# Attention and experts kernel: batch 1's reciprocals spread by 64x64 products in two banks, with a new written-out order

## The chip, the cores and the metric

The program runs on one core of one Trainium2 chip. The metric is the device time of one execution in microseconds (us); lower is better. TensorE (PE) does the matrix products, VectorE (DVE) and ScalarE (ACT) the elementwise work and everything that reads PSUM, GpSimd (POOL) elementwise work between SBUF tiles, SyncE (SP) and ScalarE issue the transfers. Each engine works through its own instructions in order.

## The reference

```python
scores = q @ k.T / 8                       # 4 batches, 12 heads, 448 rows, head size 64
scores = where(upper triangle, -1e9, scores)
attn = exp(scores - max); attn = attn / (sum(attn) + 1e-9)
x = attn @ v                               # put together: 1792 tokens x 768
h = maximum(maximum(x @ w1, x @ w2), x @ w3)
out = h @ w_out                            # all weights 768 x 768, float64 on arrival
```

## The kernel before

**Pairs.** Attention goes over 24 pairs of heads, six to a batch (`attend`, line 702; pair number u = 6b + p). A pair's score matrix is cut into seven diagonal blocks of 64 columns of queries, and these into two halves a and b. Each half is one product into a buffer S of two PSUM banks (lines 714 to 738; eight to sixteen small fp32 products in 64x64 tiles of the array, four tiles at work at once, each bank written by two of them). VectorE takes the row maxima of S (L743), a small bias is formed (L751 or L753), ScalarE takes the exponentials with the row sums (L761). There are two buffers S and three single banks M.

**Turning the exponentials.** In batch 0 ("plain") the fp32 exponentials are transposed on PE (`tr`, L774) into a bank M and copied by ScalarE to SBUF (`place`); the product with v then runs in fp32 (L847, 40 records). From batch 1 on they are split into two fp16 planes, transposed by DMA, and the product with v takes twice 30 records (L847).

**The division.** In batches 0 and 1 the product with v is divided by the row sums afterwards. The sums lie one per partition and query row, the products have queries along the free axis; so the reciprocals (L887) have to be laid along the free axis and repeated over 64 partitions. `spread` (line 896) does it on PE: stationary operand is a column of reciprocals repeated 64 times, moving operand the identity, in fp32. The result R (one bank M, 448 columns) is copied to SBUF (x32, line 914) by ScalarE and multiplied in (L906). Batches 2 and 3 divide the exponentials instead and have no spread.

**The experts.** Weights arrive as float64, are converted (`weight`: line 963 makes the first fp32 form, then three VectorE steps), scaled and split in two fp16 planes (`split`, line 1002 the high one). Hidden layers of batches 0 and 1 are products of 128x128 tiles with 448 columns, 18 to a bank M in three steps of six (L1041); batches 2 and 3 use seven combined products (L1273); L1472 and L1398 are the last projection.

**The order.** Every operation is added to a list with its engine choices; `ORDER` says in which order they are emitted and `ENGINE` which engine each takes, both written out in the file. Each engine's own sequence is that of ORDER. A buffer of a ring (S, M, ...) is claimed at an operation's place in the order and is free when its last reader is done; rings named in `FIFO` are claimed in the order of the program. PE needs a moment when the form of its tiles changes (128x128, 128x64 column halves, 64x64), which the planner calls SWITCH.

Names used below: Sa u and Sb u are pair u's score products, tr u its transposes, "product of pair u" that with v, "hidden step" six matmuls of L1041. Operation numbers up to 278 are the same in both lists; operation 216 is the last `place` of pair 5, the one that completes what the product of pair 5 (217) reads; 217 is the last product of batch 0.

Of the kernel before, what the change touches and what calls it, by code (L numbers as in the profile page):

```python
# [1618 lines left out]
```

## Time and profile before

| | |
|---|---|
| median of 3 runs | 436.22 us (436.07 to 436.66) |
| the profiled execution | 435.71 us |
| its span, first to last instruction | 433.8 us |
| granted TensorE clock, mean | 1.000 |
| PE, VectorE, ScalarE, GpSimd busy | 97%, 92%, 69%, 28% |

The profiled execution has 1.9 us around its span. In a timeline row, an instruction's duration includes its way through the pipeline, so consecutive rows overlap; what an instruction costs its engine is read from the start of one row to the start of the next. An fp32 matmul leaves two records.

### The profile page before, as it was taken

The page shows a single profiled execution, that of the slowest core. Times are in us where ns is not written, and L with a number is a line of the kernel's source. Part 1 is how long each engine was busy: PE and PEld are TensorE (multiplying, and loading weights), DVE is VectorE, ACT ScalarE, POOL GpSimd, SP SyncE. Part 2 cuts the span into 40 slices and gives each one's busy share as a digit, 9 for nine tenths or more (in the row PEclk, how much of TensorE's full clock was granted, in tenths as well). Part 3 has the DMA queues.
Part 4 walks back from the last instruction along what each step waited for, and adds up shares of the span by engine and source line. Part 5 has one row for each costly group of instructions (what it writes and reads, how often), then busy time and mean ns, then how long its engine had stood idle before and what let it go on. Part 6 is the DMA issues. An engine that isn't in the chain of part 4 may idle for free.

```text
span 433.8 us, 10850 instructions
## 1 busy us (share of the span) xinstructions
PE 422.8 (97%) x4282; PEld 244.9 (56%) x4282; DVE 400.5 (92%) x850; ACT 300.6 (69%) x738; POOL 119.7 (28%) x123
## 2 busy tenths in 40 slices
PE   7899899999999999999999999999999999999997
PEld 3677665656555555555555555565555555555554
DVE  5999999999999999996657889999999999999994
ACT  5999999789879899987679887954323422431530
POOL 3235353334452417132232332110130121121000
PEclk9999999999999999999999999999999999999999
DMA  8685589999999687587976666561000000000024
GB/s 318 233 305 196 191 244 223 236 223 220 243 259 252 164 240 133 93 162 114 204 175 156 144 143 113 98 147 38 2 0 21 2 1 23 0 2 0 0 100 155
DMA packets 87490, 60.46 MB, mean 139 GB/s; under 512 B 76304, under 2 KB 79504, under 8 KB 87440
## 3 DMA queue, kind: packets, MB, share of 16 engines
q1 hardware_dynamic: 83904, 48.14, 46.9%
q10 hardware_dynamic: 3536, 11.63, 8.1%
q8 instruction: 33, 0.54, 0.5%
q14 instruction: 17, 0.14, 0.1%
HBM read 35.39 MB, written 5.51 MB: 94 GB/s over the span
## 4 chain that ended last, share of the span: by engine, by line
PE 90%; ACT 8%; DVE 1%; issue 1%; POOL 0%; POOLq 0%; ACTq 0%
PE M L1041 29%; PE L L1273 14%; PE M L1472 10%; PE S L719 8%; PE O L847 7%; PE M L1273 7%; PE L L1398 5%; ACT region L761 4%; PE O L1273 4%; PE M L1398 2%; ACT region L541 2%; PE M L901 2%; PE O L1398 1%; ACT junk L642 1%; PE S L1532 1%; PE M L774 1%
## 5 line engine op out<-in xcount | busy, mean ns | idle before, releaser
L1041 PE MATMUL M<-x,w 128*128 128x448 f16 x648 | 127.1, 353 | 0.0
L1041 PEld LDWEIGHTS <-w 128*128 128x128 f16 x648 | 61.5, 98 | 56.8 <-issue 1.7
L761 ACT ACTIVATE region<-S,acc 128x128 f32<-128x128 f32 (+6 forms) x168 | 78.4, 480 | 9.4 <-DVE region L552 3.2
L541 ACT ACTIVATE region<-region 128x896 f16<-128x896 f32 (+3 forms) x72 | 57.7, 808 | 20.7 <-DVE region L1206 7.9
L743 DVE TENSOR_REDUCE acc<-S 128x1 f32<-128x320 f32 (+6 forms) x168 | 62.7, 416 | 9.3 <-PE S L719 8.8
L552 POOL TENSOR_TENSOR region<-region 128x896 f16<-128x896 f32 x22 | 41.5, 1890 | 52.6 <-DVE region L953 13.4
L1273 PEld LDWEIGHTS <-region 128*128 128x128 f16 x324 | 31.7, 98 | 29.6
L541 ACT ACTIVATE region<-region,cols 128x384 f16<-128x384 f32 (+1 forms) x38 | 22.6, 614 | 35.3 <-DVE region L1131 26.1
L1126 POOL TENSOR_TENSOR region<-w 128x384 f32<-128x384 f16 x21 | 19.0, 913 | 96.1 <-PE L L1273 24.9
L719 PE MATMUL S<-region 64*64 64x192 f32 (+6 forms) x672 | 43.9, 379 | 0.0
L1472 PE MATMUL M<-h,w 128*128 128x448 f16 x216 | 42.2, 353 | 0.0
L847 PE MATMUL O<-region,region 128*64 128x128 f16 (+3 forms) x1320 | 41.0, 219 | 0.0
L1273 PE MATMUL L<-region,region 128*128 128x448 f16 x189 | 37.7, 352 | 0.0
L1273 PEld LDWEIGHTS <-w 128*128 128x128 f16 x243 | 23.6, 98 | 21.9
L761 ACT ACTIVATION_READ_ACCUMULATOR region<-S,acc 128x1 f32 x168 | 35.6, 212 | 0.0
L1273 PE MATMUL M<-x,w 128*128 128x448 f16 x162 | 33.0, 353 | 0.0
L541 ACT ACTIVATE region<-region,acc 128x448 f32<-128x448 f32 (+6 forms) x59 | 28.5, 516 | 5.9 <-DVE acc L810 5.7
L1472 PEld LDWEIGHTS <-w 128*128 128x128 f16 x216 | 20.7, 98 | 19.5 <-issue 0.6
L719 PEld LDWEIGHTS S<-region 64*64 64x64 f32 x672 | 24.5, 134 | 10.8 <-issue 8.7
L847 PEld LDWEIGHTS <-region 128*64 128x64 f16 x1080 | 26.6, 111 | 5.5 <-issue 5.2
L956 DVE SCALAR_TENSOR_TENSOR region<-region 128x768 int32<-128x768 int32 x24 | 23.0, 964 | 0.0
L960 DVE SCALAR_TENSOR_TENSOR region<-region 128x768 int32<-128x768 int32 x24 | 22.8, 952 | 0.1
(174 smaller groups left out, 736.2 us busy)
## 6 DMA issues: line engine op xcount, KB each, us to landing
region<-in_moe_w_dram SPq DMA_DIRECT2D x12, 768.0 KB, 4.8
region<-in_qk_dram SPq DMA_DIRECT2D x19, 448.0 KB, 4.8
region<-in_moe_w_dram ACTq DMA_DIRECT2D x6, 768.0 KB, 4.6
region<-in_v_dram SPq DMA_DIRECT2D x10, 384.0 KB, 6.0
region<-in_moe_w_out_dram SPq DMA_DIRECT2D x4, 768.0 KB, 5.1
region<-in_qk_dram ACTq DMA_DIRECT2D x5, 448.0 KB, 4.0
...
```

The costliest lines, as they stand in the source:

```text
L541: ACT.activation(o, i, AF.Copy, scale=f)
L552: ENG[eng].tensor_tensor(out=o, in0=i, in1=hi, op=ALU.subtract)
L719: PE.matmul(ap(o, dims[0], dims[1:], D * (h ^ g), D), l, r, start=start, stop=True, skip_group_check=True)
L743: DVE.tensor_reduce(out=T(acc)[:, at : at + 1], in_=T(S)[:, c : c + w], op=ALU.max, axis=AX.X, negate=True)
L761: ACT.activation(T(y)[:, c : c + w], T(S)[:, c : c + w], AF.Exp, bias=T(acc)[:, 16 + at : 17 + at], scale=0.125, accum_out=T(acc)[:, 8 + a ...
L847: PE.matmul(o, vt(j, vl, (2 * p + h) * D), i, start=n < 2, stop=True, skip_group_check=True)
L956: DVE.scalar_tensor_tensor(out=xi(), in0=word(0), scalar=29, in1=xi(), op0=ALU.logical_shift_right, op1=ALU.bitwise_or)
L960: DVE.scalar_tensor_tensor(out=xi(), in0=word(1), scalar=SIGN, in1=xi(), op0=ALU.bitwise_and, op1=ALU.bitwise_or)
L1041: PE.matmul(T(M)[:, 0:S_LEN], w16[j][:, kk, wl, fs], xx[:, kk % 3, xl], start=(kk == 0 and wl + xl == 0), stop=(kk == 5 and wl == 1))
L1273: PE.matmul(T(M)[:, 0:S_LEN], stat(c, wl), mov(c, xl), start=first and n == 0, stop=n == 8, skip_group_check=True)
L1398: PE.matmul(T(M)[:, t[0] : t[1]], stat[0](c, wl), mov[0](c, xl)[:, t[0] : t[1]], start=first and c + wl + xl == 0, stop=c == 2 and wl == 1 ...
L1472: PE.matmul(T(M)[:, 0:S_LEN], w16[3][:, f, wl, es], T(("h", b, f))[:, hl], start=(f == 0 and hl + wl == 0), stop=(f == 5 and wl == 1))
```

## The change

For the six pairs of batch 1 the spread is done by 16 products of 64x64 tiles instead of 14 of 128x64: each takes a 64-row part of the identity and of the reciprocals, four different tiles of the array follow one another directly, and their results go to two banks of one buffer. R therefore comes from ring S (two banks) and no longer from ring M (one bank), and S is no longer in FIFO. Of the seven blocks of 64 columns one (block 3) is filled in both banks, so that both hold four. The copy to x32 becomes two instructions of 256 columns, one for each bank, with three-level patterns; the second writes block 3 over the first's. Batch 0 keeps its form.

```diff
-    FIFO = ("qk", "xr", "acc", "p32", "ph", "pT", "v16", "vr", "S", "O", "tE", "tS", "Se", "Sl", "tL")
+    FIFO = ("qk", "xr", "acc", "p32", "ph", "pT", "v16", "vr", "O", "tE", "tS", "Se", "Sl", "tL")
...
-        R, x32 = ("M", "r", b, p), ("x32", b, p)
+        R, x32 = ("M" if plain else "S", "r", b, p), ("x32", b, p)
...
         def spread(e):
             a = T(acc)
+            if not plain:
+                for k in range(4):
+                    for g, n in enumerate(((6, 4, 1, 3)[k], (5, 3, 2, 0)[k])):
+                        for h in range(2):
+                            c = D * (h ^ g)
+                            PE.matmul(
+                                ap(T(R), 512 * g + D * n, [[1, D]], D * h, D), ap(a, 24 + AT[n], [[0, D]], c, D),
+                                ident[c : c + D, c : c + D], start=True, stop=True, skip_group_check=True)
+                return
...
+        else:
+            add([("pe", 4 * c_pe32(D) + 0.03)], spread, reads=[(acc, "r")], writes=[R], ring=("S", R), prio=prio + 0.5, mode=(3, 3))
+            c = dict(act=c_act(4 * D, -0.05), dve=c_dve(4 * D))
+            for g in range(2):
+
+                def four(e, g=g):
+                    d = [[3 * D, 2], [2 * D, 2], [1, D]]
+                    scaled(e, ap(T(x32), D * (1 - g), d), ap(T(R), 512 * g + D * (1 - g), d), 1.0)
+
+                add([(e, c[e]) for e in ENGINES["R"]], four, reads=[R], writes=[x32], ring=None if g else ("xr", x32), prio=prio + 0.6)
```

Six operations are new (the second copies, five on ScalarE and one on VectorE), so the lists have 1979 entries for 1973, and numbers behind 278 move up by one to six. ORDER and ENGINE are replaced as a whole, for all batches. What the new lists say at the places that the text below comes to:

- PE's sequence from the last transposes of pair 5 on was: spread 5, hidden step, Sa 7, tr 5, tr 5, two hidden steps, product of pair 5, Sb 7, five hidden steps. It is now: tr 5, Sa 7, spread 5, tr 5, two hidden steps, product of pair 5, Sb 7, four hidden steps. One hidden step that stood ahead of the product of pair 5 now stands behind it; otherwise the same PE operations stand ahead of it.
- PE's sequence changes the form of its tiles 116 times in the old list and 123 times in the new: 40 and 38 times up to the product of pair 5, 76 and 85 times from there on.
- ScalarE's sequence up to operation 216: new in it are the first conversion of w1 (984 before, 990 now; GpSimd had it), the exponentials 266 and 267 of Sb 6 (128 and 320 columns; they stood behind 216), and the biases 125 and 253 (GpSimd and VectorE had them). No longer in it are the bias 55 (now on GpSimd) and the high plane of a weight (1033 before, 1039 now; it comes later). The sum 43 of pair 0 left for GpSimd and the sum 78 of pair 1 came from there.
- In batch 1 the spreads mostly stand alone between hidden steps, as "hidden step, spread 8, hidden step". Behind spread 6 come two hidden steps, one product for weight maxima (three matmuls), Sb 8 and then Sa 8.

## Rows read from the trace of the kernel before

**Rows 1.** The page's first part: busy us, share of the span, instructions.
```profile
PE 422.8 (97%) x4282; PEld 244.9 (56%) x4282; DVE 400.5 (92%) x850; ACT 300.6 (69%) x738; POOL 119.7 (28%) x123
```
**Rows 2.** Windows of 10 us: busy PE, PEld, DVE, ACT, POOL, clock, DMA, GB/s.
```profile
20.00:30.00 10.00, 8.86 (x135) 6.70 (x132) 9.93 (x28) 9.97 (x32) 4.18 (x7) 1.00 0.83 299
...
50.00:60.00 10.00, 10.00 (x148) 6.90 (x146) 9.93 (x22) 9.97 (x30) 4.51 (x4) 1.00 0.85 247
60.00:70.00 10.00, 10.00 (x104) 5.47 (x100) 9.93 (x21) 9.38 (x25) 3.00 (x3) 1.00 0.99 205
...
200.00:210.00 10.00, 10.00 (x133) 5.96 (x134) 5.10 (x15) 8.01 (x22) 1.66 (x3) 1.00 0.97 181
```
**Rows 3.** Waits of PE from 48 us to the end: us, times, longest.
```profile
PE M L774 <- ACT region L541: 0.8, 1, 0.8
```
**Rows 4.** Timeline of PE around batch 0's last product: start, us, what.
```profile
48.57 0.66 PE L774 MATMUL M<-ident,region 128*128 128x128 f32 x4 [0.81 <-ACT region L541]
...
52.03 1.03 PE L901 MATMUL M<-ident,acc 128*64 128x64 f32 x28
53.00 1.31 PE L1041 MATMUL M<-x,w 128*128 128x448 f16 x6
...
55.21 1.18 PE L774 MATMUL M<-ident,region 128*128 128x128 f32 x8
56.23 2.43 PE L1041 MATMUL M<-x,w 128*128 128x448 f16 x12
58.59 2.00 PE L847 MATMUL O<-region,region 128*64 128x128 f32 x40
```
**Rows 5.** Timeline of ACT ahead of that product.
```profile
46.24 0.97 ACT L541 ACTIVATE region<-region 128x768 f32<-128x768 f32 x1
47.06 0.98 ACT L541 ACTIVATE w<-region,wf 128x768 f16<-128x768 f32 x1
47.88 0.64 ACT L541 ACTIVATE region<-M 128x512 f32<-128x512 f32 x1
...
57.35 0.30 ACT L751 ACTIVATE acc<-acc,osc 128x4 f32<-128x4 f32 x1
57.54 0.60 ACT L541 ACTIVATE region<-M 128x512 f32<-128x512 f32 x1
58.01 0.38 ACT L761 ACTIVATE region<-S,acc 128x128 f32<-128x128 f32 x1
...
58.36 0.55 ACT L761 ACTIVATE region<-S,acc 128x320 f32<-128x320 f32 x1
...
58.86 0.50 ACT L761 ACTIVATE region<-S,acc 128x256 f32<-128x256 f32 x1
```
**Rows 6.** Timeline of PE in batch 1's stage.
```profile
78.42 0.25 PE L719 MATMUL S<-mr,ident 64*64 64x64 bf16 x4
78.47 0.96 PE L719 MATMUL S<-region 64*64 64x448 f32 x12
...
103.85 2.44 PE L1041 MATMUL M<-x,w 128*128 128x448 f16 x12
106.23 1.03 PE L901 MATMUL M<-ident,acc 128*64 128x64 f32 x28
107.09 0.88 PE L847 MATMUL O<-region,region 128*64 128x128 f16 x30
...
113.03 1.01 PE L901 MATMUL M<-ident,acc 128*64 128x64 f32 x28
113.97 4.71 PE L1041 MATMUL M<-x,w 128*128 128x448 f16 x24
118.52 0.22 PE L580 MATMUL M<-ident,bsc 128*128 128x128 bf16 x1
...
133.67 0.94 PE L719 MATMUL S<-region 64*64 64x128 f32 x16
134.54 1.03 PE L901 MATMUL M<-ident,acc 128*64 128x64 f32 x28
```

More of the change, by code (lines that the diff above doesn't have):

```diff
@@ L33 @@
 V_FIRST = 14
-ORDER = [15, 16, 17, 18, 19, 28, 29, 20, 977, 978, 50, 21, 30, 31, 32, 33, 0, 24, 22, 983, 23, 85, 2, 34, 979, 4, 6, 35, 51,
[94 rows of a table removed]
+ORDER = [15, 16, 17, 18, 19, 20, 28, 29, 30, 31, 983, 50, 0, 32, 984, 21, 24, 985, 33, 22, 23, 51, 986, 34, 35, 987, 36, 37,
[94 rows of a table added]
 ENGINE = (
-    "spacspdvspacpospacdvpedvdvdvdvsppedvdvdvacacacacpeacpeacpedvdvdvdvdvacacacacpeacpeacpeacdvpeacdvacposppedvdvdvac"
-    "acacacpeacpeacpedvdvdvdvpoacacacacpeacpeacpepodvpeacdvacposppedvdvdvpoacacacpeacpeacpedvdvdvdvdvacacacacpeacpeac"
-    "pepodvpeacdvacposppedvdvdvpoacacacpeacpeacpedvdvdvdvpoacacacacpeacpeacpeacdvpeacdvacposppedvdvdvpoacacacpeacpeac"
+    "spacspdvspacpospacdvpedvdvdvdvsppedvdvdvacacacacpeacpeacpedvdvdvdvdvacacacacpeacpeacpepodvpeacdvacposppedvdvdvpo"
+    "acacacpeacpeacpedvdvdvdvdvacacacacpeacpeacpeacdvpeacdvacposppedvdvdvpoacacacpeacpeacpedvdvdvdvdvacacacacpeacpeac"
+    "pepodvpeacdvacposppedvdvdvacacacacpeacpeacpedvdvdvdvpoacacacacpeacpeacpeacdvpeacdvacposppedvdvdvpoacacacpeacpeac"
@@ L134 @@
     "pedvdvdvdvacacacacacpeacpeacpepodvpeacdvacposppedvdvdvpoacacacpeacpeacpedvdvdvdvdvacacacacpeacpeacpeacdvpeacdvac"
-    "pospacspacspacspacdvpedvdvdvdvacdvacdvacdvpoacdvsppedvdvdvdvacacacacposppedvdvdvdvacacacacacacposppepeacdvpeacdv"
-    "acposppedvdvdvacacacacacposppedvdvdvdvacacacacacacposppepepodvpeacdvacposppedvdvdvacacacacacposppedvdvdvdvacacac"
-    "acacacposppepeacdvpeacdvacposppedvdvdvacacacacacposppedvdvdvdvdvacacacacacposppepeacdvpeacdvacposppedvdvdvpoacac"
-    "acacposppedvdvdvdvacacacacacacposppepeacdvpeacdvacpoacpedvdvdvacacacacacposppedvdvdvdvacacacacacacposppepeacdvpe"
@@ L139 @@
-    "acdvacpospacacacspacacacdvpedvdvdvdvacpoacdvacdvacdvacacspacspacspacdvpedvdvdvdvacpoacdvpodvpodvdvacpedvdvdvacac"
-    "acacacdvacacacacdvsppedvdvdvdvpoacacacacacdvacacacacacposppepeacdvsppedvdvdvacacacacacdvacacacacposppedvdvdvdvac"
-    "acacacacdvdvacacacacacposppepedvdvacpedvdvdvacacacacacdvacacacdvposppedvdvdvdvpoacacacacpodvacdvacdvacposppepeac"
-    "dvsppedvdvdvdvacacacpodvacdvacacposppedvdvdvdvdvacacacacacdvdvacdvdvdvdvsppepedvdvsppedvdvdvdvacacacpodvacacacac"
-    "dvsppedvdvdvdvacacacacacpodvacdvdvdvacposppepeacdvacpedvdvdvdvacacacpodvacdvdvdvdvsppedvdvdvdvacacacacacacdvacdv"
@@ L144 @@
-    "acacacdvsppepeacdvsppedvdvdvpoacacacacdvacdvdvacdvsppedvdvdvdvpoacacacacacdvdvacacacdvposppepeacdvsppedvdvdvpoac"
-    "acacdvdvacacdvacdvsppedvdvdvdvacacacacacacdvacacacacacdvsppepeacdvacpedvdvdvacacacacacdvacacacacdvsppedvdvdvdvac"
-    "acacacacpodvdvacdvdvacposppepeacdvsppedvdvdvacacacacdvdvacacdvdvdvsppedvdvdvdvacacacacacpodvdvdvacdvdvposppepeac"
-    "dvsppedvdvdvdvacacacacdvacdvacdvdvsppedvdvdvdvpoacacacacdvdvacacacacacdvsppepeacdvsppedvdvdvdvacacacacdvacacacac"
-    "dvsppedvdvdvdvacacacacacdvdvdvacacacacdvsppepeacdvsppodvdvdvdvsppodvdvdvdvsppodvdvdvdvpedvdvdvdvdvpodvpodvpoposp"
@@ L149 @@
-    "podvdvdvdvsppodvdvdvdvspacdvdvdvdvpedvdvdvdvdvacdvacdvpodvspacdvdvdvdvspacdvdvdvdvspacdvdvdvdvpedvdvdvdvdvacdvac"
-    "dvacdvacacdvdvdvdvspacdvdvdvdvacacdvdvdvdvpedvdvdvdvdvacdvacdvacdvacacdvdvdvdvacacdvdvdvdvspacdvdvdvdvpedvdvdvdv"
-    "dvacdvacdvacdvacacdvdvdvdvspacdvdvdvdvacacdvdvdvdvpedvdvdvdvdvacdvacdvacdvspacdvdvdvdvacacdvdvdvdvacacdvdvdvdvpe"
-    "dvdvdvdvacdvacdvacpospacdvdvdvdvspacdvdvdvdvspacdvdvdvdvpedvdvdvdvacdvdvdvdvdvdvacacacacacacpepepeacpepepedvpepe"
-    "pedvacpopepepeacpepepedvpepepedvacpopepepeacpepepedvpepepedvacpopepepeacpepepedvpepepedvacpopepepeacpepepedvpepe"
@@ L154 @@
-    "pedvacpopepepeacpepepedvpepepedvacpodvpepepedvsppepepeacsppepepedvsppepepeacsppepepeacsppepepeacacpepepeacpepepe"
-    "dvpepepedvacdvpepepeacpepepedvpepepedvacdvpepepeacpepepedvpepepedvacpopepepeacpepepedvpepepedvacdvpepepeacpepepe"
-    "dvpepepedvacdvpepepeacpepepedvpepepedvacpodvpepepeacsppepepeacsppepepeacsppepepeacacpepepedvacpepepeacacdvdvpopo"
-    "dvpodvdvacdvacdvpodvacdvacdvdvdvpodvdvdvacdvacdvdvpoacdvacdvdvdvdvdvdvdvacdvacdvdvdvacdvacdvdvdvdvdvdvdvacdvacdv"
-    "dvdvacdvacdvdvdvdvdvdvdvacdvacdvdvdvacdvacdvdvdvdvdvdvdvacdvacdvpodvacdvacdvpodvdvpodvdvacdvacdvdvdvacdvacdvpopo"
@@ L159 @@
-    "podvdvdvacdvacdvdvdvacdvacdvdvdvdvpodvdvacdvacdvdvdvacdvacdvpopodvdvdvdvacdvacdvpodvacdvacdvpodvpodvdvdvacdvacdv"
-    "podvacdvacdvpodvdvdvdvdvacdvacdvdvdvacdvdvdvpopopopodvdvacdvacdvdvdvacdvacdvdvpopodvdvdvacdvacdvdvdvacdvacdvpodv"
-    "podvdvdvacdvacdvdvdvacdvacdvpeacpedvpedvpedvpedvpepedvdvpeacpedvpedvpedvpedvpepedvdvdvdvdvpeacpedvpedvpedvpedvpe"
-    "pedvdvdvdvdvdvdvacdvacdvdvdvdvacdvacdvdvdvdvacdvpeacpedvpeacpedvpedvpepedvdvpeacpedvpedvpedvpedvpepedvdvdvdvdvpe"
-    "acpedvpedvpedvpedvpepedvdvdvdvdvacdvacdvacdvdvdvdvacdvacdvacdvdvdvdvpeacpedvpeacpedvpedvpepedvdvpeacpedvpedvpedv"
@@ L164 @@
-    "pedvpepedvdvdvdvdvpeacpedvpedvpedvpedvpepedvdvdvdvdvacdvacdvacdvdvdvdvacdvacdvacdvdvacdvdvpepeacpepedvpepeacsppe"
-    "pedvpepedvacpepedvacpepedvacpepeacpepedvpepeacacpepedvpepedvacpepedvsppepedvsppepeacpepedvpepeacsppepedvpepedvsp"
-    "pepedvspdvpepedvsppepedvsp")
+    "pospacspacspacspacdvpedvdvdvdvacdvacdvacdvpoacdvsppedvdvdvacacacacacposppedvdvdvdvacacacacacacposppepeacdvpeacdv"
+    "dvacposppedvdvdvpoacacacacposppedvdvdvdvacacacacacacposppepeacdvpeacacdvacposppedvdvdvacacacacacposppedvdvdvdvac"
@@ new lines @@
+    "acacacacacposppepeacdvpeacacdvacposppedvdvdvacacacacacdvsppedvdvdvdvpoacacacacacposppepeacdvpeacacdvacposppedvdv"
+    "dvpoacacacacposppedvdvdvdvpoacacacacacposppepeacdvpeacacdvacpoacpedvdvdvacacacacacposppedvdvdvdvacacacacacacposp"
+    "pepeacdvpeacacdvacpospacacacspacspacdvpedvdvdvdvacdvacdvacdvacdvspacspacspacspacdvpedvdvdvdvpodvpodvacdvacdvdvac"
+    "pedvdvdvacacacacpodvacacacacposppedvdvdvdvacacacacacacdvacacacacacposppepedvdvsppedvdvdvacacacacacdvacacacacposp"
+    "pedvdvdvdvacacacacacacdvacacacacacposppepedvdvsppedvdvdvpoacacacdvdvacacdvdvposppedvdvdvdvacacacacacacdvacacdvac"
@@ new lines @@
+    "acposppepeacdvsppedvdvdvacacacacpodvacacacacposppedvdvdvdvacacacacacacdvdvacacacacposppepeacdvsppedvdvdvacacacac"
+    "dvdvacacdvacdvsppedvdvdvdvpoacacacacdvdvacacdvacdvdvsppepedvdvsppedvdvdvacacacacdvdvacdvacacposppedvdvdvdvpoacac"
+    "acacacdvacacacdvdvdvsppepeacdvacpedvdvdvacacacacpodvdvdvdvdvdvsppedvdvdvdvacacacacacacdvdvdvacdvacdvsppepeacdvsp"
+    "pedvdvdvacacacacpodvacacacdvdvsppedvdvdvdvacacacacacacdvdvacacdvacposppepedvdvacpedvdvdvdvacacacpodvacacacdvdvsp"
+    "pedvdvdvdvacacacacacacdvacacdvacacposppepeacdvsppedvdvdvacacacacacdvacacacdvdvsppedvdvdvdvpoacacacacdvdvdvacacac"
@@ new lines @@
+    "acdvsppepedvdvsppedvdvdvdvacacacacdvacacacdvposppedvdvdvdvpoacacacacacdvacdvacacdvposppepeacdvsppedvdvdvacacacac"
+    "podvacacacacdvsppedvdvdvdvpoacacacacacdvacacacacacdvsppepeacdvsppodvdvdvdvspacdvdvdvdvsppodvdvdvdvpedvdvdvdvdvpo"
+    "dvpodvpoposppodvdvdvdvsppodvdvdvdvspacdvdvdvdvpedvdvdvdvdvacdvacdvpodvspacdvdvdvdvspacdvdvdvdvspacdvdvdvdvpedvdv"
+    "dvdvdvacpoacdvacdvacacdvdvdvdvspacdvdvdvdvacacdvdvdvdvpedvdvdvdvdvacdvacdvacdvacacdvdvdvdvacacdvdvdvdvacacdvdvdv"
+    "dvpedvdvdvdvdvacdvacdvacdvacacdvdvdvdvspacdvdvdvdvacacdvdvdvdvpedvdvdvdvdvpodvacdvacdvspacdvdvdvdvacacdvdvdvdvsp"
@@ new lines @@
+    "acdvdvdvdvpedvdvdvdvacdvacdvacpospacdvdvdvdvspacdvdvdvdvspacdvdvdvdvpedvdvdvdvacdvacdvpodvdvacacacacacacpepepeac"
+    "pepepedvpepepedvacpopepepeacpepepedvpepepedvacpopepepeacpepepedvpepepedvacpopepepeacpepepedvpepepedvacpopepepeac"
+    "pepepedvpepepedvacpopepepeacpepepedvpepepedvacdvdvpepepedvsppepepedvsppepepeacsppepepedvsppepepedvsppepepedvsppe"
+    "pepeacpepepedvpepepedvacpopepepeacpepepedvpepepedvacdvpepepeacpepepedvpepepedvacdvpepepeacpepepedvpepepedvacpope"
+    "pepeacpepepedvpepepedvacpopepepeacpepepedvpepepedvacpodvpepepeacsppepepeacacpepepeacsppepepeacsppepepeacacpepepe"
@@ new lines @@
+    "acspdvdvpodvdvpodvdvacdvacdvpodvacdvacdvpodvdvdvdvdvacdvacdvdvdvacdvacdvdvdvdvdvdvdvacdvdvdvdvdvacdvacdvdvdvpodv"
+    "dvdvacdvacdvdvdvacdvacdvdvdvdvdvdvdvacdvacdvdvdvacdvacdvdvdvdvdvdvdvdvdvacdvdvdvacdvacdvpopopopodvdvacdvacdvdvdv"
+    "acdvacdvdvdvpopodvdvacdvacdvpodvacdvacdvdvpodvpodvdvacdvacdvdvdvacdvacdvdvdvpopodvdvacdvacdvpodvacdvacdvpodvpopo"
+    "dvdvacdvacdvdvdvacdvacdvdvpodvpodvdvacdvacdvdvdvacdvacdvpodvdvdvdvdvacdvacdvdvdvacdvacdvpopopopodvdvacdvacdvdvdv"
+    "acdvacdvdvdvpopodvdvacdvacdvdvdvacdvdvdvpeacpedvpeacpedvpedvpepedvdvpedvpedvpedvpedvpedvpepedvdvdvdvdvpeacpedvpe"
@@ new lines @@
+    "dvpedvpedvpepedvdvdvdvdvacdvacdvacdvdvdvdvacdvacdvacdvdvacdvpeacpedvpeacpedvpedvpepedvdvpeacpedvpedvpedvpedvpepe"
+    "dvdvdvdvdvpeacpedvpedvpedvpedvpepedvdvdvdvdvacdvacdvacdvpodvdvacdvacdvacdvdvacdvpeacpedvpeacpedvpedvpepedvdvpeac"
+    "pedvpedvpedvpedvpepedvdvdvdvdvpeacpedvpedvpedvpedvpepedvdvdvdvdvdvdvacdvdvdvdvdvdvacdvacdvacdvdvacdvdvpepeacpepe"
+    "dvpepedvsppepedvpepedvsppepedvsppepedvsppepeacpepedvpepeacacpepedvpepedvacpepedvacpepedvsppepeacpepedvpepedvsppe"
+    "pedvpepedvacpepedvspdvpepedvsppepedvsp")
@@ L911, in attend @@
         add([("dve", 0.1)], reciprocals, reads=[(acc, "t")], writes=[(acc, "r")], prio=prio + 0.4)
-        add([("pe", 7 * c_pe32(D) + 0.09)], spread, reads=[(acc, "r")], writes=[R], ring=("M", R), prio=prio + 0.5, mode=(2, 2))
-        c = dict(act=c_act(S_LEN, 0.02), dve=c_dve(S_LEN) + 0.06)
-        add([(e, c[e]) for e in ENGINES["R"]], lambda e: scaled(e, T(x32), T(R)[:, 0:S_LEN], f),
-            reads=[R] + [("scale", b)] * plain, writes=[x32], ring=("xr", x32), prio=prio + 0.6)
+        if plain:
+            add([("pe", 7 * c_pe32(D) + 0.09)], spread, reads=[(acc, "r")], writes=[R], ring=("M", R), prio=prio + 0.5, mode=(2, 2))
+            c = dict(act=c_act(S_LEN, 0.01), dve=c_dve(S_LEN) + 0.06)
+            add([(e, c[e]) for e in ENGINES["R"]], lambda e: scaled(e, T(x32), T(R)[:, 0:S_LEN], f),
+                reads=[R, ("scale", b)], writes=[x32], ring=("xr", x32), prio=prio + 0.6)
+        else:
[6 more added lines that the diff above has]
+                add([(e, c[e]) for e in ENGINES["R"]], four, reads=[R], writes=[x32], ring=None if g else ("xr", x32), prio=prio + 0.6)
         add([("dve", c_dve(S_LEN))], quotient, reads=O_, writes=[x32], prio=prio + 0.9)
```

188 rows, old and new, of the table ORDER are left out of this document.

## The prediction

> **What bounds the kernel now.** I read the page's first part, then the busy times in windows of 10 us, then PE's waits, then the timelines of PE and ScalarE where the windows change character. The first part says only that PE and VectorE are both near full [rows 1]. The windows split the run. Until about 50 us PE has holes while VectorE and ScalarE are at 9.9 of 10: batch 0's attention needs them, and there is little else for PE to do [rows 2]. From 50 us on PE is at 10.00 in every window, and the list of its waits holds a single one after 48 us, the 0.8 us at 48.57 [rows 2, 3]. A busy PE could still be a slow one, since its durations overlap; but 24 matmuls of 448 columns start from 113.97 to 118.52, 0.190 us each, with nothing between them [rows 6]. The clock is granted in full throughout [rows 2].
>
> So the time is two things added: when PE gets into its dense stage, and how much PE work stands behind that point. ScalarE sets the first. Its queue has no gap worth the name from 20 us on [rows 2], and the last operation of batch 0 that hangs on it is the product of pair 5, which starts at 58.59, right behind two hidden steps [rows 4]. The copy that it waits for (operation 216, the ScalarE row at 57.54) ended at 57.54 + 0.60 = 58.14 [rows 5], so PE had 0.45 us in hand there. I take the start of this product as the hinge, and price what lies ahead of it and behind it apart.
>
> **Behind the hinge: the spread.** One spread of the old form takes 0.86 us when the next work has the same tile form (106.23 to 107.09) and 0.94 when it has not (113.03 to 113.97) [rows 6]. Each half of the columns streams 7 products, in two records each, of 64 columns: 896 columns in 0.86 us. A score product in four 64x64 tiles is the nearest row for the new form: one of its banks takes blocks of 128 and 320 columns, again twice, 896 columns in 0.87 us (133.67 to 134.54), while the other bank is filled beside it [rows 6]. Both give 0.97 ns a column, so the rate does not depend on the form. A tile of the new spread streams four products of 64 columns twice, 512 columns: 0.50 us. The lower bound leaves out all start-up, 0.46; the upper one, 0.60, gives the new spread one more start-up of 0.1, as weights of four tiles are changed every 64 columns and not every 128 or more. I take 0.50, the value of two rows that agree. Six spreads save 6 x (0.865 - 0.50) = 2.19 us.
>
> **Behind the hinge: changes of form.** Twelve matmuls ahead of the spread at 106.23 take 2.38 us, and 12 x 0.1896 is 2.275: entering another form costs 0.105 us; leaving it costs 0.94 - 0.865 = 0.08 [rows 6]. I take 0.095. The new list has 85 changes behind the hinge, the old one 76: 9 x 0.095 = 0.86 us lost. This is where most of the spreads are set alone between hidden steps, so that a form that they share with the scores is not used.
>
> **Behind the hinge: one step more.** One hidden step moved from ahead of the hinge to behind it, 6 x 0.1896 = 1.14 us [rows 6]. The sum behind: 1.14 + 0.86 - 2.19 = -0.19 us.
>
> **Ahead of the hinge.** PE has less to do there, 1.14 us and two changes, but ScalarE has more, and it is ScalarE that has no gap. From start to start: the conversion of w1 that comes from GpSimd 0.82 (46.24 to 47.06); the two exponentials of Sb 6 0.35 and 0.50 (58.01, 58.36, 58.86); two biases 0.19 each (57.35 to 57.54). Out of it: one bias 0.19, one high plane of a weight 0.82 (47.06 to 47.88) [rows 5]. The two sums cancel. Net +1.04 us, with perhaps 0.15 either way for rows that stand for their neighbours. The copy then ends at 59.18. PE starts 0.05 us behind such a copy (47.88 + 0.64 = 48.52, transposes at 48.57 [rows 4, 5]): the product starts at 59.23 instead of 58.59, +0.64 us. What PE is relieved of ahead of the hinge becomes idle time there.
>
> **The rest.** Two copies of 256 columns for one of 448: exponentials of 320 and 128 columns take 0.50 and 0.35 [rows 5], so some 0.8 ns a column, and 64 more columns with one more start cost ScalarE under 0.3 us a pair. ScalarE is at 9.38 in the window behind the hinge and falls to 8.01 later [rows 2], and the copied reciprocals are used only after the product with v; so nothing for it, but with that cover gone it would be 5 x 0.3 = 1.5 us at most. The one copy on VectorE (about 0.3) and VectorE's other exchanges fall where it has nearly 5 us free in a window of 10 (200 to 210) [rows 2]. The bank M that becomes free is worth nothing to a PE that does not wait [rows 3].
>
> **The sum.** +0.64 - 0.19 = +0.45 us: a span of 434.25 and a profiled execution of 436.16. The median of the runs lies 0.51 above the profiled execution; kept, that gives 436.67. With the spread at 0.46 it is 436.43, at 0.60 437.27. I forecast 436.6: no difference that can be told, since about 0.2%, 0.87 us, is what this measurement can tell from no change.
>
> **Rivals.**
> *The hinge does not move.* If the extra work on ScalarE is absorbed, or PE finds the same holes filled, only PE's work counts: 0.86 - 2.19 and two changes fewer ahead, -1.5 us, 434.7. For it speaks that PE is the bound for 380 us; against it that ScalarE's queue is full ahead of 216, so its 1.04 us cannot vanish. Chance 0.11.
>
> *Scores wait for their buffers* (slower). A spread now holds one of two buffers S until both copies are read out, and until then only one is left for scores. Behind spread 6, Sa 8 needs the second one after 0.6 + 2.37 + 0.27 + 0.84 = 4.1 us of PE work (spread, two hidden steps with a change, three matmuls for maxima, Sb 8). The spread and two copies need about 1.2 us; so it decides once ScalarE reaches these copies more than 2.9 us late, and it is at 9.38 of 10 there [rows 2]. Three such delays of 0.3 to 0.5 us give +0.9 to +1.5 on top of the sum, 437.6 to 438.2. Against it: PE had no such wait before [rows 3], though with fewer claims. Chance 0.19.
> The Trainium skill warns of this in general (TensorEngine Tiling (Array Packing), PSUM Bottleneck): tiling speeds up TensorE but not the emptying of PSUM, which may then bind. No row of the kernel before shows it here.
>
> *The change does not do what it says.* If small products are bound by their number and not by their columns, 32 records take no less than 28 did, about 0.87 us, and the sum is 6 x 0.37 higher: 438.8. The rows speak against it: four mask products in four tiles start within 0.05 us (78.42 to 78.47), 12 ns each, while the spread's 28 records take 0.86 us, 31 ns each [rows 6]. Chance 0.04.
> The Trainium skill has such a rule (TensorE: Matmul & The Clock Gate, "Wait — 56ns, not 53.3ns?"): starts are never closer than about 25 ns, however few columns. By that rule 32 records would be at least 0.80 us, an estimate. The trace disagrees for products of different tiles, with the 12 ns above.
>
> **How the numbers follow.** The sum as worked out has 0.66, and of that nearly all lies within 0.2%, with 0.05 above; the first rival 0.11 (0.10 faster), the second 0.19 (0.16 slower, 0.03 the same), the third 0.04 slower. Together: faster 0.11, the same 0.63, slower 0.26. For 8 times in 10 the range leaves out the first rival and the upper end of the second and third: 435.6 to 437.9.
>
> **What would show it.** A spread of batch 1 takes about 0.5 us and 0.1 for each change of form; the fp32 product of 40 records that ends batch 0 starts near 59.2, with a wait on ScalarE of about 1 us ahead of it; behind it PE has no wait and ends its work 0.2 us sooner than before, counted from there. I am wrong if that product starts before 58.8 (then it is faster), if PE waits for ScalarE at L719 or at the spread's line in batch 1 (the buffers), or if the spread's start to start is above 0.7 us.

## The result, and the profile after

The kernel after takes 444.23 us, the median of 11 runs (438.59 to 455.33); the kernel before, beside it on the same chips, 436.18 (435.47 to 436.77, 11 runs). The ratio is 1.0123 (95% interval 1.0100 to 1.0147), taken without the runs that lie more than 1.5% above the fastest of their kernel. So it became slower, by more than the forecast's range, and it lost its steadiness: its runs are 17 us apart, those of before 1.3, and two of the eleven took 438.6. The profiled execution took 442.60 us, with a span of 440.5.

First the page's first part, which answers to [rows 1], then windows of 10 us, to [rows 2]; columns as there. In the kernel after, L903 is the new spread, L910 that of batch 0 and L1061 the hidden step.

```profile
PE 423.1 (96%) x4306; PEld 244.3 (55%) x4306; DVE 398.9 (91%) x843; ACT 298.3 (68%) x746; POOL 125.7 (29%) x127
```
```profile
50.00:60.00 10.00, 8.42 (x131) 6.45 (x129) 9.73 (x22) 10.00 (x31) 4.84 (x4) 1.00 0.74 245
60.00:70.00 10.00, 10.00 (x127) 6.06 (x125) 9.89 (x20) 9.62 (x24) 3.12 (x3) 1.00 0.95 195
110.00:120.00 10.00, 10.00 (x147) 5.70 (x149) 9.66 (x24) 8.76 (x21) 4.37 (x3) 1.00 0.98 217
120.00:130.00 10.00, 8.03 (x119) 4.62 (x112) 9.65 (x19) 5.85 (x17) 3.34 (x3) 1.00 1.16 225
130.00:140.00 10.00, 8.53 (x87) 4.93 (x90) 6.70 (x18) 7.83 (x23) 4.54 (x5) 1.00 1.04 214
140.00:150.00 10.00, 10.00 (x101) 5.42 (x93) 9.93 (x18) 9.89 (x22) 2.41 (x2) 1.00 0.55 191
```

PE is no longer at 10.00 from 50 us on. It has a hole between 120 and 140, where VectorE and ScalarE fall as well. The list of PE's waits names what it waits for (it answers to [rows 3], over the whole span; the last line is of the kernel before).

```profile
PE S L719 <- ACT region L761: 5.3, 6, 1.5
PE O L847 <- DMA region<-region: 3.1, 1, 3.1
PE M L774 <- ACT region L541: 1.9, 3, 0.9
...
PE S L719 <- DMA region<-in_qk_dram: 0.3, 1, 0.3
```
```profile
PE S L719 <- ACT region L761: 0.4, 2, 0.2
```

The transfer from region to region is a DMA transpose, and L847 is the product of probabilities with v. The waits for ScalarE all lie ahead of 60 us; those of the score products have grown from 0.4 to 5.3 us. PE's timeline at the places that answer to [rows 4, 6]:

```profile
52.50 0.25 PE L719 MATMUL S<-mr,ident 64*64 64x128 bf16 x4 [1.45 <-ACT region L761]
...
58.56 2.43 PE L1061 MATMUL M<-x,w 128*128 128x448 f16 x12
60.92 2.00 PE L847 MATMUL O<-region,region 128*64 128x128 f32 x40
...
118.90 0.88 PE L847 MATMUL O<-region,region 128*64 128x128 f16 x30
119.71 0.69 PE L903 MATMUL S<-ident,acc 64*64 64x64 f32 x32
120.33 1.31 PE L1061 MATMUL M<-x,w 128*128 128x448 f16 x6
...
125.59 0.99 PE L719 MATMUL S<-region 64*64 64x448 f32 x12 [0.31 <-DMA region<-in_qk_dram]
126.51 0.88 PE L847 MATMUL O<-region,region 128*64 128x128 f16 x30
...
131.47 0.88 PE L847 MATMUL O<-region,region 128*64 128x128 f16 x30 [3.13 <-DMA region<-region]
```

ScalarE's timeline in the head, which answers to [rows 5]; the rows are its first bias, the last exponential of Sb 5 and copy 216:

```profile
7.54 0.30 ACT L751 ACTIVATE acc<-acc,osc 128x3 f32<-128x3 f32 x1 [5.25 <-DVE acc L743]
...
51.89 0.47 ACT L761 ACTIVATE region<-S,acc 128x192 f32<-128x192 f32 x1
...
59.92 0.61 ACT L541 ACTIVATE region<-M 128x512 f32<-128x512 f32 x1
```

The product of pair 5, the hinge, starts at 60.92, right behind two hidden steps and 0.39 us behind the end of copy 216 at 60.53: PE does not wait for that copy. Its last wait for ScalarE in the head is at 52.50, where Sb 6 needs the buffer S of Sb 5. A new spread takes 0.62 us from its start to the next work in another form; and the second product of pair 10 waits 3.13 us. From the starts of all of PE's groups, each priced by how long it takes where nothing is waited for:

| us | before | after | predicted change |
|---|---|---|---|
| start of ScalarE's first bias | 6.64 | 7.54 | 0 |
| from there to the end of copy 216 | 51.50 | 52.99 | +1.04 |
| start of the product of pair 5 | 58.59 | 60.92 | +0.64 |
| PE's work behind it | 370.85 | 370.77 | -0.19 |
| PE's waits behind it | 0 | 4.06 | 0 |
| start of PE's last operation | 430.10 | 436.66 | +0.45 |

The rest, 0.25 us, is in excesses of less than 0.06 us each. So PE's work is about what the prediction promised. The loss of this execution is 4.06 us of waits and 2.33 us in the head. Of the latter, 0.90 lie ahead of ScalarE's first bias. That bias starts anywhere from 6.60 to 7.54 us in the eighteen profiles of this case, and from 7.01 to 7.36 in the six with the new spread and the old head, so the 0.90 cannot be put down to the new order.

### The profile page after: what moved, and what is told of

Same layout as the page of the kernel before. It is cut to its first block, busy times and chain, and to the rows that moved or that the text cites. A ratio compares the mean times of both kernels' runs of the same rounds, so it can differ in the third digit from the quotient of the medians.

```text
span 440.5 us, 10891 instructions
## 1 busy us (share of the span) xinstructions
PE 423.1 (96%) x4306; PEld 244.3 (55%) x4306; DVE 398.9 (91%) x843; ACT 298.3 (68%) x746; POOL 125.7 (29%) x127
## 4 chain that ended last, share of the span: by engine, by line
PE 80%; ACT 8%; DVE 7%; DMA 2%; issue 2%; POOL 0%; ACTq 0%; DVEq 0%
PE M L1061 24%; PE L L1293 14%; PE M L1492 9%; PE M L1293 7%; PE S L719 6%; PE O L847 6%; PE L L1418 5%; ACT region L761 3%; PE O L1293 3%; ACT region L541 3%; DMA region<-region 2%; DVE acc L743 2%; PE M L1418 2%; PE O L1418 1%; DVE wmx L970 1%
## 5 line engine op out<-in xcount | busy, mean ns | idle before, releaser
L1061 PE MATMUL M<-x,w 128*128 128x448 f16 x648 | 127.8, 353 | 0.0
L1061 PEld LDWEIGHTS <-w 128*128 128x128 f16 x648 | 61.2, 98 | 55.9 <-issue 1.1
L761 ACT ACTIVATE region<-S,acc 128x384 f32<-128x384 f32 (+6 forms) x168 | 77.8, 474 | 13.0 <-POOL region L552 5.0
L541 ACT ACTIVATE region<-region 128x896 f16<-128x896 f32 (+3 forms) x69 | 55.0, 809 | 30.1 <-DVE region L1226 9.7
L743 DVE TENSOR_REDUCE acc<-S 128x1 f32<-128x448 f32 (+6 forms) x168 | 62.4, 412 | 10.8 <-PE S L719 10.6
L552 POOL TENSOR_TENSOR region<-region 128x896 f16<-128x896 f32 x24 | 45.3, 1888 | 45.4 <-ACT region L541 30.9
L719 PE MATMUL S<-region 64*64 64x384 f32 (+6 forms) x672 | 45.4, 387 | 0.3 <-DMA region<-in_qk_dram 0.3
L847 PE MATMUL O<-region,region 128*64 128x128 f16 (+3 forms) x1320 | 41.2, 219 | 3.1 <-DMA region<-region 3.1
L1146 POOL TENSOR_TENSOR region<-w 128x384 f32<-128x384 f16 x21 | 19.9, 945 | 74.1 <-DVE region L561 19.7
L761 ACT ACTIVATION_READ_ACCUMULATOR region<-S,acc 128x1 f32 x168 | 34.7, 207 | 0.0
L541 ACT ACTIVATE region<-region,acc 128x256 f32<-128x256 f32 (+6 forms) x66 | 30.3, 508 | 4.3 <-DVE acc L810 4.3
L719 PEld LDWEIGHTS S<-region 64*64 64x64 f32 x672 | 25.4, 137 | 12.1 <-issue 9.3
L847 PEld LDWEIGHTS <-region 128*64 128x64 f16 x1080 | 26.7, 111 | 8.8 <-issue 8.3
```

Of the source, the lines that this page charges most:

```text
L541: ACT.activation(o, i, AF.Copy, scale=f)
L552: ENG[eng].tensor_tensor(out=o, in0=i, in1=hi, op=ALU.subtract)
L719: PE.matmul(ap(o, dims[0], dims[1:], D * (h ^ g), D), l, r, start=start, stop=True, skip_group_check=True)
L743: DVE.tensor_reduce(out=T(acc)[:, at : at + 1], in_=T(S)[:, c : c + w], op=ALU.max, axis=AX.X, negate=True)
L761: ACT.activation(T(y)[:, c : c + w], T(S)[:, c : c + w], AF.Exp, bias=T(acc)[:, 16 + at : 17 + at], scale=0.125, accum_out=T(acc)[:, 8 + a ...
L847: PE.matmul(o, vt(j, vl, (2 * p + h) * D), i, start=n < 2, stop=True, skip_group_check=True)
```

## The experiments

The first theory was that the new order costs, by its waits for transposes and by its head, and not the new form. The rival was that the claims on the buffers S cost. The edits below are written as sequences: a13 and b13 stand for Sa 13 and Sb 13 and what hangs on them, o10 for the product of pair 10 with its spread and copies, h3 for a hidden step. In the kernels of several experiments every line stands one higher up: L846 there is L847 here.

What PE loses behind the hinge is counted as in the table above: its waits, and with them what the products take longer at a lower granted clock.

**The new spread in the old order (e1), and the old products in the new order (e2).**

```diff
 e1: ORDER and ENGINE of the kernel before, the second copy behind the first
-    [PE] o10 spread, h3, h4 ...              [PE] a13, b13, o11 spread
+    [PE] h3, h4 ..., o10 spread, h4          [PE] o11 spread, a13, b13
 e2:
-    ap(T(R), 512 * g + D * n, [[1, D]], D * h, D), ap(a, 24 + AT[n], [[0, D]], c, D), ident[c : c + D, c : c + D]
+    T(R)[D * h : D * h + D, 512 * g + D * n : ...], ap(a, 24 + AT[n], [[0, D]]), ident[:, c : c + D]   # 7 n, as before
```

> The order and the engines of the kernel before, with the new spread, its buffer S and its two copies; where the old place would lock the two buffers S (pairs 10 and 11) spread and copies are moved by a few instructions. The first theory (the new order is what costs: its products stand closer behind the DMA transposes that they read, and its head feeds ScalarE later) expects no loss: six spreads 2.0 us shorter, two changes of form more (118 for 116, 0.19 us), so about 434.4 us, 433.6 to 435.2, the product of pair 5 at 58.6 in the span and no wait of PE for a transpose. The rival (the new form costs: the scores wait for the buffers S that spreads hold) expects waits of 0.3 to 1 us at the score products L719 behind most spreads and 437.5 us or more.

> The kernel after with the seven products of the old form (128 rows, 64 columns each) in place of the sixteen 64x64 ones; order, engines, buffers S and the two copies stay. The first theory (the order costs) expects the loss to stay and the saving to go: about 0.25 us more per spread, 1.5 us in all, so 440 to 457 us with a median near 445, and the product of pair 5 near 60 to 61 in the span. The rival that the 64x64 form itself costs expects 438 us or less.

e1 took 449.3 us (446.8 to 451.5, ratio 1.030, 1.024 to 1.035), e2 440.2 (439.5 to 446.4; 1.009, 1.006 to 1.011). In e1 PE loses 13.2 us behind the hinge, of which 10.3 are waits. e1 refutes the first theory in the form in which I put it down: the old order with the new spread is worse than the new one. PE's waits from 60 us on in e1, then ScalarE's timeline in the longest:

```profile
PE S L719 <- ACT region L761: 5.3, 1, 5.3
PE S L903 <- ACT region L761: 3.6, 2, 3.0
PE S L719 <- ACT region L541: 0.8, 2, 0.6
PE S L903 <- DVE acc L810: 0.6, 1, 0.6
```
```profile
76.41 0.31 ACT L761 ACTIVATE region<-S,acc 128x64 f32<-128x64 f32 x1
...
81.33 0.94 ACT L541 ACTIVATE region<-region 128x768 f32<-128x768 f32 x1 [4.51 <-DVE w L561]
...
82.58 0.80 ACT L541 ACTIVATE region<-S 128x256 f32<-128x256 f32 x2 [0.31 <-issue]
```

The spread of pair 6 starts at 70.86 and holds a buffer S; its copies on ScalarE come at 82.58, behind a weight's conversion that itself waited 4.51 us. Sa 8 holds the other buffer until its last exponential (76.41), and Sb 8 waits 5.31 us for it. This is the second rival of the prediction, in the old order. In the new order the copies stand close behind the spreads, and the one wait for a buffer S behind the head is 0.29 us (Sa 8, 72.73). e2's PE work is 1.76 us longer than that of the kernel after; 6 x 0.335 less three changes of form at 0.095 is 1.73. The saving is real, and without the new form 3.8 us of the loss stay.

**The two halves crossed: old head (e3), new head (e4).** Both are put together at the product of pair 5.

```diff
 e3
-ORDER = after[: product of pair 5] + after[...]
+ORDER = before[: product of pair 5] + after[...]
 e4
+ORDER = after[: product of pair 5] + e1[...]
```

> The kernel after, but all that stands ahead of the product of pair 5 in the order (and its engines) as before; behind it the new order. If the loss is in the part behind (products that wait for DMA transposes, 4.1 us of waits in the profile after), the product of pair 5 is back at 58.6 and the time is some 2 us under that of the kernel after and still well above 436: 439 to 450, with waits of several us for transposes. If the loss is in the head, the time is 434 to 436.

> The counterpart: the head of the kernel after, and behind the product of pair 5 the order of the kernel before, with the new spread. If the loss is in the part behind, that product starts at 60 to 61 in the span, nothing waits behind it, and the time is 436.2 + 1.5 to 2.3 - 1.8 = 436 to 437. If it is in the head it is 441 or more.

e3: 441.6 us (438.2 to 452.1). Its profile is that of the 452.1: there the transposes of pair 10 took 13.9 and 19.0 us, and PE lost 15.7 us behind the hinge, of which 11.7 are waits. The product of pair 5 is not back at 58.6 there, as expected, but at 59.93; the first bias starts at 7.36, and the granted clock is 0.50 from 9.6 to 13.0 us. e4: 452.4 us, with a loss of 17.9 us, mostly in the places of e1 and none of it at a transpose (11.7 are waits, and the granted clock is 0.50 for 13.6 us behind two of them); copy 216 ends 52.95 us after the first bias, against 51.50 in e1. So the head loses 1.4 us whatever follows it, and the waits for transposes belong to the new order behind it. e3's profile also shows one reason why the runs differ by so much. Its windows (the granted clock stands third from the end), then its timeline behind the second wait:

```profile
134.00:137.00 3.00, 0.00 (x0) 0.00 (x0) 0.54 (x2) 0.00 (x0) 0.00 (x0) 0.81 1.11 102
137.00:140.00 3.00, 0.48 (x12) 0.48 (x13) 0.00 (x0) 0.50 (x1) 0.00 (x0) 0.50 0.96 366
...
143.00:144.00 1.00, 1.00 (x7) 0.52 (x6) 1.00 (x3) 0.92 (x6) 1.00 (x1) 1.00 0.88 191
```
```profile
139.52 1.49 PE L846 MATMUL O<-region,region 128*64 128x128 f16 x30 [6.15 <-DMA region<-region]
140.94 5.37 PE L1060 MATMUL M<-x,w 128*128 128x448 f16 x23
```

While PE stands still, the granted clock falls to 0.50 (1.2 GHz for 2.4) and is back at 1.00 only from 143 us on, and the product behind the wait takes 1.42 us from start to start instead of 0.81. Such a wait is paid for twice. In the profile of the kernel after, the clock stayed at 1.00 through the wait of 3.13 us; over its eleven runs the mean granted clock goes from 1.000 (438.6 us) to 0.981 (455.3).

**Which transfer? (e5, e10, e11, e14, e6)** In the kernel after, the transfers of pair 10 stand like this: load of weight 16 issued at 112.08, first transpose 115.07, q and k of pair 12 at 116.50, second transpose 120.43, weight 17 at 122.62.

```diff
 [ScalarE's queue]  e10 (e5 makes the second move too, e11 that alone)
   load of weight 15
+  load of q and k of pair 12
   h0 high plane, a10 and b10 high planes, ..., a11 exponentials
-  load of q and k of pair 12
   conversion of weight 16, ..., b11 exponentials
-  load of weight 17                    (e5, e11)
   a11 high plane, o10 copy, h4, o11 sums
+  load of weight 17                    (e5, e11)
 e14: load of q and k of pair 12 behind the bias of b11 instead
 e6 (kernel before): the same load from before the first to behind the second exponential of a11
```

> The kernel after with two loads moved on ScalarE's queue, so that they don't run beside the two DMA transposes of pair 10: that of q and k of pair 12 up to right behind the load of weight 15, that of weight 17 down behind the sums of pair 11. Nothing else. The theory (transposes and loads that run beside each other slow each other down: 10.7 and 11.0 us from issue to landing in the profile after, 6.9 and 4.3 before) expects both transposes to land within 4 to 8 us, the products of pair 10 to wait less than 0.5 us instead of 3.8, and 437 to 441 us with less spread from run to run. The rival (the transposes are late because what feeds them, or the queue ahead of them, is late; the loads beside them are innocent) expects transposes of 9 us or more again, waits of 3 us or more, and 442 to 452 us.

> The kernel after with the load of q and k of pair 12 alone moved away from the first transpose of pair 10 (issued right behind the load of weight 15); the load of weight 17 stays beside the second one. If each load slows the transpose beside it, the first transpose lands within 8 us and the second still takes 8 us or more, so the second product of pair 10 waits 1 to 3 us. If the first slow transpose is what starts it all, since the second queues behind it, both are back at 4 to 8 us and nothing waits there.

> The kernel after with the load of weight 17 alone moved behind the second transpose of pair 10. If each load slows the transpose beside it, the first one takes 10 to 12 us as in the kernel after, together with the load of q and k, and the second one 5 to 8 us, so that the second product waits 0 to 1.5 us instead of 3.2. If the weight's load is innocent, the second takes 10 us or more again and the wait stays at 3 us.

> The kernel after with the load of q and k of pair 12 moved the other way, some 3 us later on ScalarE's queue, behind the bias of Sb 11. If any load beside a transpose is slow, both transposes of pair 10 or the second one take 8 us or more again and waits of 3 us or more stay, 441 to 450. If only the moment counts (issued right behind the first transpose while the load of weight 16 still runs), both land within 8 us; Sa 12 then waits up to 2 us for its q and k, and the time is 438 to 440.5.

> The reverse test: the kernel before with a single DMA issue moved, the load of q and k of pair 12, from before the first to behind the second exponential of Sa 11 on ScalarE's queue, some 3.4 us later, so that it runs beside the second transpose of pair 10. If loads beside transposes are what slows both, that transpose takes 7 to 11 us from issue to landing instead of 4.3, the load 7 us or more instead of 4.6, and PE waits 2 us or more there: 438.5 to 442 us. If they don't disturb each other, the load lands at about 122.3, PE waits for it 0.5 us, and the time is 436.2 to 437.

| | us (range) | transposes of pair 10, issue to landing | that load | PE's loss behind the hinge |
|---|---|---|---|---|
| before | 436.2 | 6.9, 4.3 | 4.6 | 0 |
| after | 444.2 (438.6 to 455.3) | 10.7, 11.0 | 9.1 | 4.06 |
| e5 both loads | 440.9 (440.3 to 444.3) | 7.5, 4.3 | 5.1 | 3.41 |
| e10 q and k alone | 438.0 (437.7 to 438.2) | 6.2, 4.5 | 5.1 | 0.29 |
| e11 weight alone | 443.3 (441.6 to 444.9) | 13.6, 10.2 | 12.4 | 7.52 |
| e14 q and k later | 439.6 (439.3 to 440.0) | 5.7, 8.2 | 3.8 | 1.45 |
| e6 before, later | 436.2 (435.4 to 437.5) | 5.5, 5.2 | 3.8 | 0.39 |

e10 settles the cause behind the hinge: one DMA issue, made 5 us earlier, takes away all of it but 0.29 us, and the two runs are 0.5 us apart. The same move stands in e5, e8, e15 and e17, and in none of them does a transpose of pair 10 take more than 7.5 us. It is the load of q and k, not that of weight 17: e11 moves the weight alone and keeps the loss (Sa 12 waits 3.8 us for its q and k, and the granted clock falls to 0.50), and e5, which moves both, pays 1.4 us at hidden steps that wait for weights, 0.7 at Sa 12 and 0.4 at the spread of pair 11, both for ScalarE. The DMA issues from 111 to 126 us (queue, KB each, median us from issue to landing), of e10 and then of the kernel after:

```profile
region<-in_moe_w_dram ACTq DMA_DIRECT2D x1, 768.0 KB, 4.7
region<-in_qk_dram ACTq DMA_DIRECT2D x1, 448.0 KB, 5.1
region<-region SPq DMA_TRANSPOSE x2, 5.3
```
```profile
region<-in_moe_w_dram ACTq DMA_DIRECT2D x1, 768.0 KB, 8.5
region<-in_qk_dram ACTq DMA_DIRECT2D x1, 448.0 KB, 9.1
region<-region SPq DMA_TRANSPOSE x2, 10.8
```

And what the DMA engines of the kernel after did from 119.3 to 125.7 us, in 40 slices (busy tenths, GB/s):

```profile
DMA  9998999999989999999939744225389966698999
GB/s 314 282 280 56 102 93 93 93 90 70 163 203 296 304 125 51 85 42 157 117 45 336 72 35 30 27 29 22 24 290 298 248 246 246 247 183 198 205 293 288
```

In several stretches the engines are at 9 of 10 or more while they move 42 to 102 GB/s; in e10 the same window shows 184 to 294 in most slices up to the landing of the second transpose. But a load beside a transpose is not enough: in the kernel before and in e6 the same load runs beside one and neither suffers (e6 was a weak test: ScalarE's queue issued the load 1.5 us later, not the 3.4 that I expected). e14 lies between, and neither of its two expectations holds in full: the load itself is quick, the second transpose takes 8.2. The five kernels that show the slow pair (after, e2, e3, e7, e11) issue the load 1.0 to 1.8 us behind the first transpose. The kernel before issues it 2.0 us behind, and e12, e13 and e16 within 0.02 us of it, with weight 16 still on its way as well; there the transpose takes 5.9 to 7.4 us and the load 3.9 to 5.5. What makes the moment between bad stays open. So does what the kernel after's two runs of 438.6 us did there, of which no trace was kept.

**The products later (e7), and everything together (e8).**

```diff
 [PE]  e7, e8 (e8 also has the old head and the two moves of e5)
   o10 first product, b12
+  h3, h3, h3
   o10 second product
-  h3, h3, h3
```

> The kernel after with the three hidden steps that follow the second product of pair 10 with v put ahead of it, so that its transpose has 3.4 us more. The loads stay as they are. If that product's wait (3.2 us) is all that is lost behind the head, the time falls by 3 us against the kernel after: 439 to 442 us, median near 441. If late transposes cost in other places too (ScalarE's high planes of pair 11, which wait for the buffers that the transposes read), the wait comes back further on and less than 1.5 us is won: 442 to 450.

> All together: the head of the kernel before, behind it the order of the kernel after with the two loads moved away from the transposes and the three hidden steps put ahead of the second product of pair 10. If loads beside transposes and the head are the whole loss, the product of pair 5 starts at 59 in the span, PE waits less than 1 us behind it, and the six spreads show their saving: 435 to 436.5 us, the same as before or a little under. If the new order has other weak places, 438 or more with waits elsewhere.

e7: 444.7 us (442.2 to 447.7). The second product loses 0.31 us instead of 3.2, but the transposes are as slow (11.1, 12.3), and PE waits 1.0 at Sa 12 for its q and k and 2.1 at a product for weight maxima (L579) further on. ScalarE's high planes of pair 11 need the buffers that the transposes read and wait for them, in e7 as long as this:

```profile
133.10 0.95 ACT L540 ACTIVATE region<-region 128x896 f16<-128x896 f32 x1 [4.34 <-DMA region<-region]
```

Behind them ScalarE's conversion of a weight is late, then VectorE's maxima of it, and then PE. The wait only moves. e8: 441.1 us (440.3 to 442.1), with a loss of 5.6 us: 2.3 at the joint with the old head (60 to 73 us), where PE arrives earlier and waits above all for ScalarE, the rest in places of e5 and at the maxima of e7.

**The head (e15, e17).** In the kernel after, ScalarE has two gaps ahead of exponentials that wait for a bias on GpSimd. The timelines of ScalarE, GpSimd and VectorE, in this order:

```profile
13.32 0.63 ACT L761 ACTIVATE region<-S,acc 128x448 f32<-128x448 f32 x1 [0.34 <-POOL acc L753]
...
31.76 0.37 ACT L761 ACTIVATE region<-S,acc 128x128 f32<-128x128 f32 x1 [0.43 <-POOL acc L753]
...
12.38 0.91 POOL L753 TENSOR_SCALAR acc<-acc 128x3 f32<-128x3 f32 x1 [0.80 <-DVE acc L743]
20.84 0.19 POOL L753 TENSOR_SCALAR acc<-acc 128x3 f32<-128x3 f32 x1 [6.12 <-DVE acc L743]
30.72 1.00 POOL L753 TENSOR_SCALAR acc<-acc 128x4 f32<-128x4 f32 x1
...
12.32 0.91 DVE L980 SCALAR_TENSOR_TENSOR region<-region 128x768 int32<-128x768 int32 x1
```

```diff
 both on top of e10
 e15: -ENGINE[conversion of w1] = act    +pool
 e17: -ENGINE[bias of a1, bias of b3] = pool    +dve
```

> The kernel after with the load of q and k of pair 12 issued early (as in the run that gave 438.0) and the conversion of w1 back on GpSimd; the biases stay where they are. If ScalarE's added 0.82 us of conversion is what delays the head, the product of pair 5 starts 0.6 to 0.9 us earlier (59.0 plus what the first score product loses to a late clock, for 59.8), 437.2 us. If the waits on GpSimd's biases set it, nothing is won, or it is slower since GpSimd has more: 438 to 439.

> The kernel after with the load of q and k of pair 12 issued early and the biases of Sa 1 and Sb 3 on VectorE instead of GpSimd. If ScalarE's two gaps (0.34 and 0.42 us) are lost time of the head, its stretch from the first bias to copy 216 falls from 52.9 to 52.2 or 52.4 us, the product of pair 5 starts 0.5 us earlier, 437.4 us. If other work sets the head, the stretch stays at 52.8 or more and the time at 438.0.

e15: 438.6 us (437.9 to 438.8), no gain. ScalarE loses 0.82 us of work, but the gaps in its stretch grow by 0.9 us and the stretch from 52.91 to 53.31. How much of these gaps is the move's own is not shown: in this profile the granted clock is 0.50 from 9.5 to 12.9 us. e17: 437.5 us (436.6 to 443.5, 10 runs; ratio 1.0037, 1.0014 to 1.0060). The stretch is 51.90 us, 1.01 shorter than in e10; its gaps are 0.75 us less, and the exponential follows the copy ahead of it without a gap (ScalarE's timeline of e17, then VectorE's, with the bias):

```profile
12.16 0.62 ACT L540 ACTIVATE region<-M 128x512 f32<-128x512 f32 x1
12.63 0.67 ACT L760 ACTIVATE region<-S,acc 128x448 f32<-128x448 f32 x1
...
12.12 0.17 DVE L752 TENSOR_SCALAR acc<-acc 128x3 f32<-128x3 f32 x1
```

So 1.0 of the head's 1.4 us hung on two biases on GpSimd, one of them moved there by the change.

**A better place for the spreads in the old order (e12, e13, e16).**

```diff
 e12 on e1
   [ScalarE] o6 copies behind b7's high plane; o8 copies behind b9's, o11's behind b12's scaling; o7's ahead of b8's bias
   [PE] b8 behind three h1 steps; o7 spread ahead of a9; b13 behind o11's first product
 e13 on e12: o6 spread one h1 step later; [VectorE] two maxima of b8 and o7's reciprocals behind weight 9
 e16 on e12: o6 spread one h1 step later; [VectorE] weight 9's third step ahead of those maxima, o7's reciprocals right behind them
```

> The old order with the new spread again, now with spreads, copies and some scores put where a buffer S is free: the two copies of pair 6 behind b7's high plane and Sb 8 three hidden steps later, the spread of pair 7 ahead of Sa 9, the copies of pairs 8 and 11 earlier on ScalarE, Sb 13 behind pair 11's first product. 122 changes of form for 116. If the waits of the first experiment came from buffers S held while ScalarE was busy with other work, and the spread itself is as fast as in the kernel after, PE waits less than 1 us behind the product of pair 5 and the time is 436.2 - 2.0 + 0.6 = 434.8, 434.2 to 435.6 us. If the claims cost whatever the place, waits of several us stay and the time is over 437.

> The old order with moved spreads, with its two waits mended: the spread of pair 6 one hidden step later, and on VectorE two maxima of Sb 8 and the reciprocals of pair 7 put so that no maximum waits for a score product that is now later. If the spread's saving is real and the buffers S cost only by their places, PE waits under 0.6 us behind the product of pair 5 and the time is 436.2 - 2.0 + 0.6 + 0.3 = 435.1, 434.5 to 436 us. If claims of S cost anyhow, waits of 2 us or more come up in other places: 437.5 or more.

> The old order with moved spreads once more: as in the version that gave 438.2, with the spread of pair 6 one hidden step later and, on VectorE, only the last step of weight 9 put ahead of two maxima of Sb 8 and the reciprocals of pair 7 right behind them. If its two waits (0.7 and 2.2 us) were all that was lost, 435.5 to 436.3 us, the same as before or just under. If moving one wait only makes the next, 437.5 or more.

438.2 us (437.5 to 444.0), 438.9 (437.6 to 439.4) and 439.4 (438.2 to 441.2). e12 cuts e1's loss behind the hinge from 13.2 to 2.9 us by placing alone, and most of that is at two spreads; but mending those two only made others (4.3 us in e13, 3.6 in e16, the longest of them 1.5 and 2.2 at Sb 9 for a buffer S). In none of the three did the saving show. No version that was run beats the kernel before; e17 comes nearest, at 437.5 against 436.3 beside it.

## Why the prediction was wrong

- **Spread, right.** 0.62 from start to start, less 0.095 for the change of form, is 0.53; I took 0.50 out of 0.46 to 0.60. The saving is 2.0 us, predicted 2.19. That 32 records fit into 0.53 us, 17 ns each, also decides the last rival. The Trainium skill's floor of some 25 ns between starts (TensorE: Matmul & The Clock Gate, "Wait — 56ns, not 53.3ns?") would make it 0.80, an estimate; the trace disagrees.
- **Changes of form and the hidden step, right.** PE's work behind the hinge changed by -0.08 us for -0.19.
- **"The product starts at 59.23 instead of 58.59": a step that failed.** It starts at 60.92, 2.33 us later and not 0.64; three terms make the difference. First, 0.90 lie at the very start: the first score products take 1.77 us for 0.99, the granted clock reads 1.00 in both kernels there, and the runs show no cause (the expectation of e15 calls it a late clock; no row shows one). Second, ScalarE's stretch grew by 1.49, not 1.04: its work grew less than I summed (+0.8), but 0.65 of gaps came in. I had booked a bias that moves to GpSimd as 0.19 us saved on ScalarE, and had not asked who waits for it there. Third, I let the product start 0.05 us behind copy 216, so that the 0.45 us that PE had in hand there would be used up. But the product waits for that copy in neither kernel, and stands 0.38 to 0.46 us behind it in all eighteen profiles. PE's last wait for ScalarE ends at 48.57 before and at 52.50 after, at Sb 6; from there it works for 10.02 and 8.42 us up to the hinge. ScalarE does set the hinge, but in the kernel after through an exponential that frees a buffer S, and not through the copy.
- **"Behind it PE has no wait": this step failed**, and it decides. It was carried over from the kernel before, with no look at which transfers the new order sets beside each other. The order moved the transposes of pair 10 and the loads around them by 1.5 to 3.9 us, and so against one another: the load of q and k of pair 12 came from 2.0 to 1.4 us behind the first transpose. I priced instructions of PE and ScalarE alone. In its place the runs show 4.06 us of waits, most of it at Sa 12 and at the second product of pair 10, and e10, with that load issued 5 us earlier, has 0.29.
- **The rival with the buffers S** does not happen in the kernel after (0.29 us), though e1 and e4 show that it is real: 13 and 18 us in the old order, the slower products behind the waits included. The new order avoids most of that, and e12 avoids most of it in the old order by placing alone.
